# Loading the local attention's values 64 keys at a time for all heads, with the scores put to match and every step in a new order

## The chip, the cores and the metric

The kernel runs on one core of a Trainium2 chip. The metric is the device time of one execution in microseconds (us). The version before the change has a median of 604.21 us over three runs (601.29 to 608.74). One further execution was recorded by the hardware profiler; every duration of a single instruction below comes from that one.

The core has a matrix engine (PE), three elementwise engines (DVE, ACT and POOL) and a queue called SP, which in this kernel issues every DMA transfer. Each of the five works through its own instructions strictly in order, and waits on semaphores when an input is not there yet.

## What is computed

Two pieces follow one another: an attention with a pooled and a local part, and a feed-forward block (the "FFN").

```python
B, H, S, D = 8, 8, 576, 64
# pooled part: q, k, v averaged over 4 neighbouring positions
out_d  = softmax(q_d @ k_d.T / 8) @ v_d            # 144 x 144 a head
# local part: only keys with |i - j| < 4 count
scores = where(mask, q @ k.T / 8, -1e9)
out    = repeat(out_d, 4) + softmax(scores) @ v
x      = out.transpose(0, 2, 1, 3).reshape(4608, 512)
# FFN
h  = x @ w_in                                      # 512 -> 1024
so = h * softmax(h)
ln = (so - mean(so)) / sqrt(var(so) + 1e-6) * g_ln
return ln @ w_out                                  # 1024 -> 512
```

The weights arrive as 64-bit floats and are turned into 32-bit ones on the core.

## The kernel before

**Attention, local part.** The 576 query positions of a batch are cut into ten windows of 64 keys, and two neighbouring windows make a unit `u` (five units a batch). All eight heads of a unit are worked on together, as four pairs of heads (`pr`), each with an even and an odd head (`par`). In batches 0 to 2, and for the fifth unit of batches 3 to 7, class `Local` (L525) does one unit: scores on PE (L539), mask, maximum, subtraction, exp, sum and scaling on DVE, POOL and ACT, a transpose of the probabilities through PE (L580), a copy out of PSUM (L583), the product with v on PE (L590) and the addition to the output (L595). That makes 15 + 5 = 20 units. In batches 3 to 7 the first four units go through class `PairOfLocals` (L601), two units at once, whose probabilities are transposed by DMA and DVE.

**How v is laid out for it.** `load_vw` (L256) fills one tile of 128 partitions for a unit; there are five such buffers. For a `Local` unit it uses four transfers of 64 KB: the half of the partitions is `par ^ wi` (`wi` is the window, 0 or 1), so that each half holds the even heads of one window and the odd heads of the other. The scores are laid out to suit: row half `wi`, PSUM bank `par ^ wi`; after the transpose the row half is `par ^ wi`. For the units of `PairOfLocals` the same function already uses two transfers of 128 KB, one for each window, with all eight heads side by side; there the row half is the window.

**Attention, pooled part.** Class `Pooled` (L698) works on the averaged q, k and v; v for it is loaded by `load_vs` and `load_tail` (L274, L284) and summed by L451 and L454.

**FFN.** The 4608 rows are cut into 36 tiles of 128 rows. For a tile, `ffn_in` (L773) makes 24 matmuls of 512 columns into one PSUM buffer (L779; high and low parts of weights and rows, three products), then maximum (L787), exp (L791), product (L794), centring (L817 on ACT or L819 on DVE), a store to DRAM (L827, `u`) and a sum of squares on ACT (L836), which waits for that store. `ffn_back` (L853) reads it back in four transfers (L859, `v`), `ffn_ut` transposes it on DVE (L880) and splits it (L886, L889), and `ffn_out` (L896) makes 24 more matmuls into another single PSUM buffer (L903), which ACT empties (L910). The last tile transposes on PE instead.

**Weights.** Sixteen pieces of 512 KB are loaded by `Weights.load` (L325, the steps `wload`) and converted by ACT (L334), DVE (L340 to L349) and DVE or POOL.

**The order.** The kernel first lists all its work as 1847 numbered steps (`step` and `row`, L948 to L953). A step is a piece of one unit or tile: one group of matmuls, one elementwise operation, or one load. They are then issued in the sequence of the list `ORDER` (L26), so this list alone sets the order of every engine's queue, SP's too. A second list, `OTHER` (L116), names the steps that run on the second-choice engine instead of the usual one (DVE in place of POOL or ACT; for the clamp at L336 POOL in place of DVE).

Some step numbers, for following the order in the code:

| step | what it is |
|---|---|
| 237, 245, 253, 261 | loads of the weight pieces 12, 13, 14, 15 |
| 238 | first conversion step of weight piece 12 (ACT, L334) |
| 278 | store of FFN tile 0 (L827) |
| 407, 417 | v load of batch 1, unit 0; the product on PE that reads it |
| 1249, 1263 | v load of batch 5, unit 0; the product on PE that reads it |
| 1677, 1692 | v load of batch 7, unit 3; the product on PE that reads it |
| 1445, 1446 | q and k load of batch 6, pair 1; the first DVE transpose that reads it |

Of the kernel before, what the change touches and what calls it, by code (L numbers as in the profile page):

```python
# [10 lines left out]
F32 = mybir.dt.float32  # L11
# [113 lines left out]
def pooled_local_attention_then_solu_ffn(  # L125
# [10 lines left out]
    nc = tc.nc  # L136
    P = 128
# [16 lines left out]
    W = 64  # L154
# [17 lines left out]
    def rows(n):  # L172
        return slice(n * 64, n * 64 + 64)
# [891 lines left out]
```

## Time and profile before

| quantity | value |
|---|---|
| median of three runs | 604.21 us (601.29 to 608.74) |
| the profiled execution, its own time | 605.33 us |
| its span from first to last instruction | 603.5 us |
| mean granted PE clock over the span | 0.963 |
| ACT busy | 306.1 us |
| POOL busy | 308.1 us |
| DMA issues, all on SP | 732 |
| data moved by DMA | 99.70 MB |

The profiled execution lies 1.12 us above the median; 605.33 - 603.5 = 1.8 us of it lie around the span. Busy time counts an engine's own work; issuing a DMA is not counted as busy, so SP's load is read from its timeline. In a timeline row the first number is the start in us after the span's start, the second the time the merged instructions take, and a bracket at the end gives the idle time of that engine before it, with the instruction or transfer that ended it. "PEclk" or "granted clock" is the share of full speed that PE was given.

### The profile page before, as it was taken

To read this page: it belongs to the slowest core of one execution; us is meant where nothing else is said; L and a number is where in the kernel's file an instruction comes from. 1 tells how busy PE (TensorE), PEld (TensorE's weight loads), DVE (VectorE), ACT (ScalarE), POOL (GpSimd) and SP (SyncE) were. 2 spreads that over 40 slices of the span, in tenths; PEclk is the share of its full clock that TensorE was granted. 3 is DMA by queue.
4 is the path that set the end of the run, shared out by engine and by line. 5 is a ranking of instruction groups with operands and counts; after the bars stand their busy time and mean duration, and the time that the engine had idled before them with its cause. 6 is when DMAs were issued, how large, how long until landed. Compare 5 with 4: busy or idle time off the path is not lost.

```text
span 603.5 us, 16899 instructions
## 1 busy us (share of the span) xinstructions
PE 560.4 (93%) x6728; PEld 436.9 (72%) x6728; DVE 459.0 (76%) x716; ACT 306.1 (51%) x639; POOL 308.1 (51%) x457
## 2 busy tenths in 40 slices
PE   7877978799899999979989999998999999999996
PEld 4655656577677777757767777776877777787885
DVE  3999987999787888768877876777888867654641
ACT  2466763576544564544534654454534547342443
POOL 5476574657385374554635564544637523532111
PEclk9698998799899999989998999998999999999999
DMA  8998658876878677797587877667672642333230
GB/s 237 243 233 147 136 123 171 210 185 136 189 182 161 194 205 206 136 250 185 153 216 155 207 206 168 160 164 183 182 196 77 200 136 81 107 122 123 88 123 35
DMA packets 208271, 99.70 MB, mean 165 GB/s; under 512 B 164288, under 2 KB 194496, under 8 KB 208192
## 3 DMA queue, kind: packets, MB, share of 16 engines
q1 hardware_dynamic: 208192, 98.62, 65.1%
q8 instruction: 53, 0.87, 0.6%
q14 instruction: 26, 0.21, 0.1%
HBM read 65.54 MB, written 27.79 MB: 155 GB/s over the span
## 4 chain that ended last, share of the span: by engine, by line
PE 42%; DVE 16%; SPq 16%; DMA 12%; issue 6%; POOL 5%; ACT 2%; DVEq 0%; POOLq 0%; ACTq 0%
PE h L779 18%; PE o L903 18%; SPq L249 6%; SPq L666 4%; DMA w<-in_moe_w_out_dram 2%; DMA stage<-in_moe_w_in_dram 2%; SPq L859 2%; PE po L755 2%; DMA v<-u 2%; SPq L268 2%; DMA qm<-in_q_dram 1%; DVE nmx L787 1%; DMA u<-e 1%; DVE kd L381 1%; PE sd L717 1%
## 5 line engine op out<-in xcount | busy, mean ns | idle before, releaser
L903 PE MATMUL o<-wo_h,uh 128*128 128x512 f32 x288 | 118.1, 410 | 5.4 <-ACT osb L910 5.4
L779 PE MATMUL h<-wi_h,xh 128*128 128x512 f32 x288 | 119.7, 416 | 1.4 <-DVE e L794 1.4
L779 PE MATMUL h<-wi_l,xh 128*128 128x512 f32 x288 | 116.6, 405 | 0.0
L779 PE MATMUL h<-wi_h,xl 128*128 128x512 f32 x288 | 116.3, 404 | 0.0
L903 PE MATMUL o<-wo_l,uh 128*128 128x512 f32 x288 | 115.0, 399 | 0.0
L889 POOL TENSOR_TENSOR ul<-v,uh 128x512 fp32r<-128x512 f32 x46 | 60.8, 1325 | 53.2 <-ACT uh L886 41.9
L903 PE MATMUL o<-wo_h,ul 128*128 128x512 f32 x288 | 79.5, 398 | 0.0
L791 ACT ACTIVATE e<-h,nmx 128x1024 f32<-128x1024 f32 x36 | 40.1, 1115 | 68.4 <-DVE nmx L787 64.2
L903 PEld LDWEIGHTS o<-wo_h,uh 128*128 128x128 f32 x288 | 54.7, 190 | 21.0 <-ACT osb L910 6.2
L779 PEld LDWEIGHTS h<-wi_h,xh 128*128 128x128 f32 x288 | 56.0, 194 | 16.7 <-DVE e L794 2.0
L880 DVE STREAM_TRANSPOSE v<-v 128x512 f32<-128x512 f32 x70 | 46.5, 690 | 25.6 <-DMA v<-u 24.5
L779 PEld LDWEIGHTS h<-wi_h,xl 128*128 128x128 f32 x288 | 55.9, 194 | 14.0 <-DVE xl L937 0.3
L779 PEld LDWEIGHTS h<-wi_l,xh 128*128 128x128 f32 x288 | 56.0, 194 | 12.4
L903 PEld LDWEIGHTS o<-wo_h,ul 128*128 128x128 f32 x288 | 54.7, 190 | 13.3
L886 ACT ACTIVATE uh<-v 128x512 fp32r<-128x512 f32 x70 | 42.9, 623 | 41.0 <-DVE v L880 21.9
L903 PEld LDWEIGHTS o<-wo_l,uh 128*128 128x128 f32 x288 | 54.8, 190 | 11.9
L787 DVE TENSOR_REDUCE nmx<-h 128x1 f32<-128x1024 f32 x36 | 43.6, 1211 | 24.5 <-PE h L779 24.5
L794 DVE SCALAR_TENSOR_TENSOR e<-h,e 128x1024 f32<-128x1024 f32 x36 | 43.6, 1212 | 14.4 <-ACT e L791 14.4
L799 POOL TENSOR_SCALAR nmu<-su 128x1 f32<-128x1 f32 x36 | 8.5, 237 | 76.9 <-DVE e L794 75.7
L836 ACT ACTIVATE e<-e 128x1024 f32<-128x1024 f32 x35 | 36.8, 1052 | 20.5 <-DMA u<-e 20.5
L817 ACT ACTIVATE e<-e,nmu 128x1024 f32<-128x1024 f32 x24 | 27.6, 1148 | 32.2 <-POOL nmu L799 32.2
L910 ACT ACTIVATE osb<-o,s 128x512 f32<-128x512 f32 x36 | 24.5, 679 | 32.3 <-PE o L903 13.5
(122 smaller groups left out, 1042.7 us busy)
## 6 DMA issues: line engine op xcount, KB each, us to landing
u<-e SPq DMA_DIRECT2D x35, 512.0 KB, 3.3
v<-u SPq DMA_DIRECT2D x140, 128.0 KB, 3.4
out_dram<-osb SPq DMA_DIRECT2D x36, 256.0 KB, 2.9
vs<-in_v_dram SPq DMA_DIRECT2D x64, 128.0 KB, 3.6
qm<-in_q_dram SPq DMA_DIRECT2D x96, 72.0 KB, 2.9
km<-in_k_dram SPq DMA_DIRECT2D x96, 72.0 KB, 2.5
vw<-in_v_dram SPq DMA_DIRECT2D x80, 64.0 KB, 2.9
vw<-in_v_dram SPq DMA_DIRECT2D x40, 128.0 KB, 3.3
```

The source lines that it names most:

```text
L249: nc.sync.dma_start(t[nm][Q * 32:Q * 32 + 32, pr], src[b, 2 * pr + par, :, dh * 32:dh * 32 + 32].rearrange("(k t) d -> t k d", t=32),)
L779: nc.tensor.matmul(hps[:, n, :], src[:, cc, :], wt[:, cc, n * 512:(n + 1) * 512], start=(cc == 0 and src is xh and wt is wi_h), stop=(cc = ...
L787: nc.vector.tensor_reduce(out=nmx, in_=hf, op=ALU.max, axis=AX.X, negate=True)
L791: nc.scalar.activation(e, hf, AF.Exp, bias=nmx, scale=1.0, accum_out=se)
L794: nc.vector.scalar_tensor_tensor(out=e, in0=hf, scalar=1.0, in1=e, op0=ALU.mult, op1=ALU.mult, accum_out=su)
L817: nc.scalar.activation(e, e, AF.Identity, bias=nmu, scale=1.0)
L836: nc.scalar.activation(e0, e, AF.Square, accum_out=m2)
L880: nc.vector.transpose(vg, vg)
L886: nc.scalar.activation(uh, tp, AF.Copy)
L889: (usual if v is None else engine(usual, nc.vector)).tensor_tensor(out=ul, in0=tp, in1=uh.bitcast(F32), op=ALU.subtract)
L903: nc.tensor.matmul(o, src[:, j, :], wt[:, 4 * g + j, :], start=(g == 0 and j == 0 and src is uh and wt is wo_h), stop=(g == 1 and j == 3 a ...
L910: nc.scalar.activation(osb, o, AF.Copy, scale=s)
```

## The change

Three things change; the arithmetic doesn't.

First, `load_vw` always uses two transfers of 128 KB, one a window, with all eight heads side by side. For the 20 `Local` units this takes two transfers where there were four: 732 DMA issues in all become 692. The bytes stay the same, and so does the run of 256 bytes (one head's 64 values of one key) that each element of a transfer covers.

Second, the scores of a `Local` unit go to row half `par ^ wi` and PSUM bank `wi` (before: row half `wi`, bank `par ^ wi`), and the product with v reads row half `wi`. The number and size of the matmuls stay.

Third, `ORDER` is another sequence of the same 1847 steps, and `OTHER` another choice (79 steps where there were 78, of which 25 are in both).

```diff
     def load_vw(b, u):
-        vw = load.tile([P, 2, NPR, D], F32, tag="vw", name=f"vw_{b}_{u}", bufs=5)
-        if b >= PAIRED and u < 4:
-            vw = vw.rearrange("p a r d -> p (a r) d")
-            for wi in range(2):
-                s0 = starts[2 * u + wi]
-                nc.sync.dma_start(vw[rows(wi)], v[b, :, s0:s0 + W, :].rearrange("h s d -> s h d"))
-            return vw
-
-        for par in range(2):
-            for wi in range(2):
-                s0 = starts[2 * u + wi]
-                nc.sync.dma_start(
-                    vw[rows(par ^ wi), wi, :, :],
-                    v[b, par::2, s0:s0 + W, :].rearrange("h s d -> s h d"),
-                )
+        vw = load.tile([P, H, D], F32, tag="vw", name=f"vw_{b}_{u}", bufs=5)
+        for wi in range(2):
+            s0 = starts[2 * u + wi]
+            nc.sync.dma_start(vw[rows(wi)], v[b, :, s0:s0 + W, :].rearrange("h s d -> s h d"))
         return vw
...
                     nc.tensor.matmul(
-                        sc[rows(wi), par ^ wi, pr * W:(pr + 1) * W],
+                        sc[rows(par ^ wi), wi, pr * W:(pr + 1) * W],
                         bt.qT[rows(par), pr, s0:s0 + W], bt.kT[rows(par), pr, s0:s0 + W],
...
             for pr in range(NPR):
-                for row, par in TILES:
-                    wi = row ^ par
+                for wi, par in TILES:
                     nc.tensor.matmul(
-                        xp[rows(par), wi, pr, :], bt.vw[u][rows(row), wi, pr, :],
-                        plT[rows(row), pr, wi, a0[wi]:a0[wi] + nw], start=True, stop=True,
+                        xp[rows(par), wi, pr, :], bt.vw[u][rows(wi), 2 * pr + par, :],
+                        plT[rows(wi), pr, par ^ wi, a0[wi]:a0[wi] + nw], start=True, stop=True,
                     )
```

Of the two lists, which fill some hundred lines, these places matter below.

- Ahead of the load of weight piece 12 (step 237), SP has 98 DMA issues before the change and 49 after it; ahead of piece 15 (step 261) 103 and 34, of piece 14 (step 253) 128 and 65, of piece 13 (step 245) 133 and 116.
- PE has 318 steps in its queue; 243 of them stand within two places of where they stood, and the last 16 are the same in both.
- At the head of the list the loads of two weight pieces now stand ahead of the first load of q; before it was one.
- The v load of batch 5, unit 0 (step 1249) stands directly ahead of the product that reads it (step 1263), where 180 steps lay between them; that of batch 7, unit 3 (step 1677) three steps ahead of its product (step 1692), where 317 lay between; and the q and k load of batch 6, pair 1 (step 1445) directly ahead of its first transpose (step 1446), where 42 lay between.
- In `OTHER`, DVE gains five accumulations, four scalings of pair units, three scalings of the pooled part, two centrings, two clamps of weights and one scaling of a single unit, and loses four copies of transposed probabilities, two subtractions of pair units, one of a single unit, two sums of v, two low parts of FFN rows and one copy of q.

180 rows, old and new, of tables (ORDER, OTHER) are left out of this document.

## The prediction

> **What bounds the kernel now.** I read the page's busy shares first, then busy time by stage, then SP's, DVE's and ACT's timelines in the stage that stood out. From the page:
>
> ```profile
> span 603.5 us, 16899 instructions
> ...
> PE 560.4 (93%) x6728; PEld 436.9 (72%) x6728; DVE 459.0 (76%) x716; ACT 306.1 (51%) x639; POOL 308.1 (51%) x457
> ...
> DMA packets 208271, 99.70 MB, mean 165 GB/s; under 512 B 164288, under 2 KB 194496, under 8 KB 208192
> ...
> PE 42%; DVE 16%; SPq 16%; DMA 12%; issue 6%; POOL 5%; ACT 2%; DVEq 0%; POOLq 0%; ACTq 0%
> ```
>
> PE is 93% busy, so over the whole span at most 43 us of idle PE can be won. But the chain that ended last spends 16% of the span in SP's queue, issuing transfers. Where, the windows tell (time, then busy us of PE, weight loads, DVE, ACT, POOL; granted clock, DMA share, GB/s):
>
> ```profile
> 0.00:75.00 75.00, 60.17 (x1131) 44.01 (x1134) 63.58 (x108) 40.09 (x93) 43.46 (x46) 0.91 0.86 199
> 75.00:125.00 50.00, 39.92 (x562) 29.45 (x553) 42.33 (x67) 26.89 (x45) 30.76 (x35) 0.86 0.72 164
> 125.00:470.00 345.00, 332.06 (x4054) 261.19 (x4054) 277.09 (x425) 178.96 (x385) 192.89 (x284) 0.98 0.73 178
> 470.00:592.00 122.00, 121.86 (x971) 97.60 (x970) 74.56 (x116) 56.69 (x112) 39.65 (x89) 1.00 0.37 120
> 592.00:603.50 11.50, 6.37 (x29) 4.68 (x27) 1.45 (x3) 3.50 (x6) 1.32 (x5) 1.00 0.12 46
> ```
>
> From 125 us on PE is the bound: 12.9 us idle of 345, then 0.1 of 122. Since its work is fixed and its queue is full, whatever is won before 125 us is kept to the end. Before 125 us DVE is the busiest engine. From 75 to 125 PE lacks 10.1 us and DVE 7.7. What DVE waits for there:
>
> ```profile
> 90.75 1.22 DVE L794 SCALAR_TENSOR_TENSOR e<-h,e 128x1024 f32<-128x1024 f32 x1 [1.93 <-ACT e L791]
> ...
> 95.81 0.43 DVE L336 TENSOR_SCALAR w<-w 128x512 f32<-128x512 f32 x1 [3.83 <-ACT w L334]
> ...
> 115.83 0.43 DVE L336 TENSOR_SCALAR w<-w 128x512 f32<-128x512 f32 x1 [0.89 <-ACT w L334]
> ```
>
> These are 1.93 + 3.83 + 0.89 = 6.65 of the 7.7 us. ACT, which ends all three, waits in turn for DMA:
>
> ```profile
> 88.47 1.06 ACT L836 ACTIVATE e<-e 128x1024 f32<-128x1024 f32 x1 [2.87 <-DMA u<-e]
> ...
> 95.11 0.67 ACT L334 ACTIVATE w<-w 128x512 f32<-128x512 f32 x1 [3.39 <-DMA w<-in_moe_w_out_dram]
> ```
>
> The first holds back ACT's exp (L791), and through it DVE's L794. And the transfers are late because SP issues without a pause; here are its rows:
>
> ```profile
> 59.35 5.83 SPq L268 DMA_DIRECT2D vw<-in_v_dram  x8
> ...
> 75.67 9.68 SPq L268 DMA_DIRECT2D vw<-in_v_dram  x12
> 85.45 0.55 SPq L827 DMA_DIRECT2D u<-e  x1
> 86.09 2.61 SPq L268 DMA_DIRECT2D vw<-in_v_dram  x4
> 88.80 0.55 SPq L325 DMA_DIRECT2D w<-in_moe_w_out_dram  x1
> ...
> 91.34 0.38 SPq L325 DMA_DIRECT2D w<-in_moe_w_out_dram  x1
> 91.81 4.49 SPq L268 DMA_DIRECT2D vw<-in_v_dram  x4
> ...
> 109.50 0.60 SPq L325 DMA_DIRECT2D w<-in_moe_w_out_dram  x1
> ```
>
> Twelve v issues take 9.68 us ahead of the store of tile 0 at 85.45, four more stand ahead of a weight load at 88.80, and four (91.81) ahead of the one at 109.50. PE itself waits for v once:
>
> ```profile
> 89.09 0.37 PE L590 MATMUL xp<-plT,vw 64*64 64x58 f32 x2 [2.71 <-DMA vw<-in_v_dram]
> 90.17 1.43 PE L590 MATMUL xp<-plT,vw 64*64 64x58 f32 x30 [0.72 <-DMA vw<-in_v_dram]
> ```
>
> **The change, part by part. Fewer issues.** Issue durations (min/median/max in ns) of the 64 KB loads, then of the 128 KB loads that the other units have already:
>
> ```profile
> L268 SPq DMA_DIRECT2D vw<-in_v_dram x80: 595/615/1921, 30.8 to 456.1; - x80
> ```
>
> ```profile
> L262 SPq DMA_DIRECT2D vw<-in_v_dram x40: 595/634/2392, 197.1 to 472.8; - x40
> ```
>
> A larger transfer costs SP nearly the same, so a unit falls from 4 x 0.615 = 2.46 us to 2 x 0.634 = 1.27: 1.19 less, and 20 units give 23.8 us of SP time. In the rows above, from 59.35 to 88.70, stand 24 v issues, which are six units: SP would reach the weight load at 88.80 some 6 x 1.19 = 7.1 us earlier and, with five units by then, the store at 85.45 some 5.9 us earlier. Each is more than the wait that hangs on it (3.83 and 1.93), and by 109.50 the seven units of these rows have saved 8.3 us against 0.89. Moreover the new order puts weight pieces 12, 15 and 14 at 49, 34 and 65 issues from the head of SP's queue instead of 98, 103 and 128. So I let all three waits of DVE go: -6.65 us. What is late next is DVE's own work, which fills the rest of this stage (42.33 + 6.65 = 48.98 of 50 us), so PE can't win its whole 10.1 us. The bounds are 0 (something else ends these waits) and -10.1 (all of PE's idle time). PE's own 3.4 us for v lie at the same place as DVE's first two waits and are not added.
>
> The Trainium skill ("DMA: Bandwidth & Descriptors", section "Issuing engines are not separate DMA queues") says that sequencer time for starting transfers is usually small beside the transfer. By it this part is worth about nothing, and the time would stay at 604.2. The rows decide against it for this stage, where SP's issues stand back to back and other transfers queue behind them; the case is the first rival below.
>
> **Transfers themselves.** Time to landing of the larger loads, from the page's list of issues:
>
> ```profile
> vw<-in_v_dram SPq DMA_DIRECT2D x40, 128.0 KB, 3.3
> ```
>
> Bytes and 256-byte runs stay. I take 0, since v is loaded ahead of its use; where that cover is gone, PE waits for the issues and these 3.3 us, which is the last rival.
>
> **Scores put to match.** Two rows of the chain (start, us, what):
>
> ```profile
> 137.07 1.09 PE sc L539 x64
> ...
> 144.40 0.92 PE sd L717 x48
> ```
>
> Two score steps take 1.09 us, 17 ns a matmul record. In the new layout neighbouring matmuls use different row halves of PE but the same column half. The pooled scores (L717) already do that, at 19 ns a record with 144 columns instead of 64, so I take 0. If such neighbours did wait for each other a step would double: 20 x 0.55 = 11 us, a bound I hold unlikely. No row speaks for a gain: the 17 ns are already under L717's 19.
>
> **The second-choice list.** Counted over the list DVE has 17 steps more and 12 fewer. The largest kind is the scaling of a pair unit on DVE:
>
> ```profile
> L656 DVE TENSOR_TENSOR pl<-pl,mxl 128x1024 f32<-128x1024 f32 x2 | 2.4, 1208 | 0.0
> ```
>
> Five net steps at no more than 1.21 us are at most +6 us of DVE work over the whole kernel. In the part of the list that runs up to 125 us it is one step fewer, and after 125 us DVE is idle 345 - 277 = 68 us: cost 0, and +6 if that cover were gone.
>
> **The new order.** PE's queue hardly moves (243 of 318 steps within two places), so its work ahead of each FFN tile is the same. At the head, one more 512 KB weight load stands ahead of the first q: 0.52 MB at 199 GB/s is 2.6 us that q comes later, or that DVE starts converting weights earlier; I take 0, bounds +2.6 and -2.6. After 125 us the 12.9 us of PE idle and, at clock 0.98, some 7 us of slower clock are stalls that a new order may heal or make. I see no sign which, and take 0; bounds -20 (all healed) and +21 (three new stalls, priced below).
>
> **Sum.** 603.5 - 6.65 = 596.9 us of span, 605.33 - 6.65 = 598.7 for this execution; it lay 1.1 above the median, so against the median 604.21 - 6.65 = 597.6 us.
>
> **The rivals.** *Nothing comes of it, 604.2 us.* The waits end with transfers, not with their issue: if the DMA engines are the limit, the same bytes land as late as before. For it: the DMA share of 0.86 up to 75 us, and 164288 of 208271 packets under 512 B, which stay. The Trainium skill (the same page, "Specifications") asks for at least 512 B a transfer to reach line rate, and this change leaves 256. Against it: the share is only 0.72 from 75 to 125, and SP, not a transfer, is what the late store and weights queue behind.
>
> *The steady stage heals too, about 587.6 us.* A freer SP queue, 10 issues fewer after 200 us, and a new order remove half of the 20 us of stalls and slow clock: 597.6 - 10 = 587.6. From 5.5 us on it is faster by over 2%. For it: SP's 16% of the chain is more than this one stage. Against it: only 10 of the 40 issues lie there.
>
> *Loads too close to their use, 616.8 us.* Steps 1249, 1677 and 1445 now stand right ahead of what reads them. If SP is no longer ahead there, PE waits for two issues and the landing, 1.27 + 3.3 = 4.6 us, and the slower clock adds 7 / 12.9 of that: 7.0 us. Less what such a stall would overlap, 6.4. Three of them give 597.6 + 3 x 6.4 = 616.8; one alone leaves the forecast, two bring back the time before, the third decides. For it: the wait at 89.09 is such a case (step 407 stood three places ahead of 417). Against it: SP often runs ahead of the list's place, and three must miss.
>
> **How the numbers follow.** Forecast (start stage wins, steady stage as before) 0.52, its own range 592 to 603; nothing comes of it 0.18; steady stage heals 0.16; loads too close 0.14, of which over half stays below the third stall. About 2% (592.1 and 616.3) is what a measurement of this kernel can tell from no change. Faster by over 2%: 0.16 and a sliver of the forecast, 0.17. Slower: 0.06 of the last rival and 0.02 for doubled score steps, 0.08. Within: 0.75. The range 588 to 611 leaves out about half of the second and half of the third rival.
>
> **What would show it.** Right: 20 units with two v issues of about 0.63 us; DVE's waits on ACT L334 and L791 between 75 and 125 us gone, and its busy time there near 49 of 50 us; the stage from which PE is over 95% busy begins near 118 instead of 125 us; L539 still 1.09 us for two steps. Wrong: PE stalls on v in batches 5 or 7, DVE waiting on batch 6's k, or weights still late behind other transfers.

## The result and the profile after

The changed kernel takes 577.07 us (median of four runs, 576.53 to 577.40), the kernel before 604.56 us beside it (601.29 to 608.74). The ratio is 0.954, with a 95% interval of 0.948 to 0.960: faster, by some 27 us where 6.65 had been forecast. The time lies below the predicted range. The profiled execution took 576.97 us with a span of 575.2 us and a mean granted clock of 0.991.

From the page of the changed kernel:

```profile
span 575.2 us, 16860 instructions
...
PE 544.7 (95%) x6728; PEld 422.1 (73%) x6728; DVE 460.3 (80%) x720; ACT 304.2 (53%) x637; POOL 303.5 (53%) x455
...
DMA packets 207631, 99.70 MB, mean 173 GB/s; under 512 B 163648, under 2 KB 193856, under 8 KB 207552
...
PE 78%; DVE 8%; DMA 5%; SPq 4%; issue 2%; ACT 2%; POOL 1%; POOLq 0%; DVEq 0%; ACTq 0%
```

SP's queue has gone from 16% to 4% of the chain that ended last. The span fell by 603.5 - 575.2 = 28.3 us. Of these, 560.4 - 544.7 = 15.7 us are PE's busy time, with the same 6728 matmuls: they ran at a higher clock. The other 12.6 us are idle time of PE.

Where it went, by stage of the changed kernel (columns as in the prediction: time, then busy us of PE, weight loads, DVE, ACT, POOL; granted clock, DMA share, GB/s):

```profile
0.00:75.00 75.00, 55.96 (x1122) 39.53 (x1126) 62.94 (x109) 41.52 (x94) 40.37 (x44) 0.93 0.95 222
75.00:125.00 50.00, 44.05 (x719) 32.66 (x709) 47.70 (x80) 35.84 (x69) 37.27 (x42) 1.00 0.83 186
125.00:470.00 345.00, 344.20 (x4209) 270.14 (x4208) 295.40 (x447) 182.52 (x390) 198.65 (x304) 1.00 0.72 181
470.00:563.00 93.00, 92.95 (x664) 74.16 (x663) 52.84 (x85) 40.58 (x80) 26.12 (x64) 1.00 0.35 117
```

Two stages won. From 75 to 125 us DVE works 47.70 of 50 us where it worked 42.33, and PE 44.05 where it worked 39.92. From 125 to 470 us PE lacks 0.80 us of 345 at clock 1.00, where it lacked 12.94 at 0.98. The prediction had put a gain on the first stage and none on the second.

In the first stage, DVE's waits for ACT's conversions and exp are gone from the timeline. Of idle times before DVE's rows, the timeline from 75 to 125 us shows only one, for another reason:

```profile
116.77 0.71 DVE L868 STREAM_TRANSPOSE v<-v 128x512 f32<-128x512 f32 x1 [1.65 <-DMA v<-u]
```

In the second stage, the view of waits from 125 to 470 us names what PE waited for (us in total, times, longest). Before:

```profile
PE o L903 <- ACT osb L910: 4.1, 1, 4.1
PE sc L620 <- DVE qT L427: 2.4, 2, 1.5
PE po L755 <- POOL vd L454: 2.3, 1, 2.3
PE po L755 <- DVE pd L746: 1.6, 1, 1.6
PE h L779 <- DVE e L794: 1.1, 1, 1.1
PE sd L717 <- DVE pl L626: 1.1, 1, 1.1
...
```

After:

```profile
PE sc L608 <- DVE pl L614: 0.3, 1, 0.3
PE sc L608 <- DVE r L818: 0.3, 1, 0.3
PE plt L569 <- DVE pl L560: 0.2, 1, 0.2
```

The stalls of over 1 us had six different causes, so no single engine or transfer was at fault. What else changed shows one step further back, in DVE's waits in the same stretch. Those for DMA before:

```profile
DVE v L880 <- DMA v<-u: 19.2, 10, 3.8
DVE kT L423 <- DMA km<-in_k_dram: 8.2, 3, 4.1
...
DVE plT L671 <- DMA plT<-pl: 5.6, 3, 2.1
```

and after:

```profile
DVE v L868 <- DMA v<-u: 1.8, 1, 1.8
```

Before, DVE waits 33.0 us here for transfers, 19.2 of them for FFN tiles on their way back to the transposes. In the changed kernel it waits 1.8 us. ACT's waits for the stores of these tiles, before it squares them, fall too; first before, then after:

```profile
ACT e L836 <- DMA u<-e: 16.0, 7, 5.6
```

```profile
ACT e L824 <- DMA u<-e: 1.2, 1, 1.2
```

Whether these waits are the cause is the question of the last experiments.

**A measure used below.** PE's order hardly differs between the kernels, so their progress can be compared at equal work. PE's lag at a mark of 120 us is the time at which it starts the step that has 120 us of PE's own work before it in the queue, less 120; each step counts at the duration it has at full clock. The mark of 120 is reached at 156.4 us before the change and at 146.6 after it, so what is lost up to it belongs to the start; what the lag grows from 120 to 500 belongs to the steady stage. Only differences between kernels are read from it: the lag of the changed kernel grows by 14.8 us too, though its PE is idle for only 0.80 us between 125 and 470 us, so most of that growth is in the way the steps are counted and no loss.

### The profile page after: what moved, and what is told of

It reads as the page before. It is cut to its first block, busy times and chain, and to the rows that moved or that the text cites. A ratio compares the mean times of both kernels' runs of the same rounds, so it can differ in the third digit from the quotient of the medians.

```text
span 575.2 us, 16860 instructions
## 1 busy us (share of the span) xinstructions
PE 544.7 (95%) x6728; PEld 422.1 (73%) x6728; DVE 460.3 (80%) x720; ACT 304.2 (53%) x637; POOL 303.5 (53%) x455
## 2 busy tenths in 40 slices
DMA packets 207631, 99.70 MB, mean 173 GB/s; under 512 B 163648, under 2 KB 193856, under 8 KB 207552
## 4 chain that ended last, share of the span: by engine, by line
PE 78%; DVE 8%; DMA 5%; SPq 4%; issue 2%; ACT 2%; POOL 1%; POOLq 0%; DVEq 0%; ACTq 0%
PE o L891 32%; PE h L767 30%; SPq L249 3%; PE po L743 3%; PE xp L666 2%; DMA km<-in_k_dram 2%; PE sc L608 2%; PE sd L705 2%; DMA qm<-in_q_dram 1%; PE qp L485 1%; PE plt L569 1%; PE warm L948 1%; PE kp L485 1%; PE xp L578 1%; DVE w L334 1%
## 5 line engine op out<-in xcount | busy, mean ns | idle before, releaser
L767 PE MATMUL h<-wi_h,xh 128*128 128x512 f32 x288 | 116.7, 405 | 0.3 <-DVE e L782 0.3
L767 PE MATMUL h<-wi_h,xl 128*128 128x512 f32 x288 | 113.9, 396 | 0.0
L767 PE MATMUL h<-wi_l,xh 128*128 128x512 f32 x288 | 113.9, 395 | 0.0
L877 POOL TENSOR_TENSOR ul<-v,uh 128x512 fp32r<-128x512 f32 x48 | 64.1, 1340 | 42.2 <-ACT uh L874 35.4
L767 PEld LDWEIGHTS h<-wi_h,xh 128*128 128x128 f32 x288 | 54.1, 188 | 14.6 <-issue 0.9
L891 PEld LDWEIGHTS o<-wo_h,ul 128*128 128x128 f32 x288 | 53.8, 188 | 14.1 <-POOL ul L877 0.9
L767 PEld LDWEIGHTS h<-wi_h,xl 128*128 128x128 f32 x288 | 54.1, 188 | 13.2 <-POOL xl L925 0.2
L767 PEld LDWEIGHTS h<-wi_l,xh 128*128 128x128 f32 x288 | 54.1, 188 | 12.0
L898 ACT ACTIVATE osb<-o,s 128x512 f32<-128x512 f32 x36 | 24.5, 680 | 50.1 <-PE o L891 16.9
L925 POOL TENSOR_TENSOR xl<-x,xh 128x512 fp32r<-128x512 f32 (+1 forms) x26 | 32.0, 1233 | 21.1 <-ACT xh L922 20.7
L805 ACT ACTIVATE e<-e,nmu 128x1024 f32<-128x1024 f32 x22 | 25.2, 1146 | 22.5 <-POOL nmu L787 22.5
```

What stands on the lines that cost most here:

```text
L767: nc.tensor.matmul(hps[:, n, :], src[:, cc, :], wt[:, cc, n * 512:(n + 1) * 512], start=(cc == 0 and src is xh and wt is wi_h), stop=(cc = ...
L805: nc.scalar.activation(e, e, AF.Identity, bias=nmu, scale=1.0)
L877: (usual if v is None else engine(usual, nc.vector)).tensor_tensor(out=ul, in0=tp, in1=uh.bitcast(F32), op=ALU.subtract)
L891: nc.tensor.matmul(o, src[:, j, :], wt[:, 4 * g + j, :], start=(g == 0 and j == 0 and src is uh and wt is wo_h), stop=(g == 1 and j == 3 a ...
L898: nc.scalar.activation(osb, o, AF.Copy, scale=s)
L925: engine(nc.gpsimd, nc.vector).tensor_tensor(out=l, in0=src, in1=h.bitcast(F32), op=ALU.subtract)
```

## Experiments

All times are medians; the ratio is to runs of the kernel before on the same chip (603 to 607 us), with its 95% interval. The last two columns are PE's lag as just described, from each one's profiled execution.

| kernel | us | ratio | lag at 120 | growth 120 to 500 |
|---|---|---|---|---|
| before | 604.56 | 1 | 36.4 | 33.2 |
| changed | 577.07 | 0.954 [0.948, 0.960] | 26.6 | 14.8 |
| e1, loads and layout alone | 592.59 | 0.983 [0.979, 0.988] | 31.1 | 25.6 |
| e2, order and layout, four loads | 588.09 | 0.976 [0.971, 0.981] | 37.4 | 15.7 |
| e3, order alone | 588.25 | 0.977 [0.972, 0.983] | 36.6 | 15.9 |
| e4, new order, old `OTHER` | 612.07 | 1.017 [1.011, 1.022] | 32.5 | 43.6 |
| e5, SP's queue from the new order | 643.68 | 1.062 [1.055, 1.069] | 33.9 | 73.4 |
| e6, SP's queue from the old order | 658.26 | 1.088 [1.082, 1.094] | 39.6 | 82.4 |
| e7, old order, new `OTHER` | 610.01 | 1.008 [1.005, 1.012] | 34.5 | 39.7 |
| e8, one load moved | 592.84 | 0.978 [0.973, 0.983] | 31.4 | 27.8 |
| e9, old head, new rest | 582.68 | 0.960 [0.955, 0.966] | 32.6 | 15.1 |
| e10, new head, old rest | 589.52 | 0.973 [0.969, 0.977] | 29.5 | 25.2 |
| e11, old half, new rest | 586.64 | 0.968 [0.964, 0.972] | 30.3 | 21.2 |
| e12, q ahead of a weight | 579.85 | 0.961 [0.956, 0.965] | 28.5 | 14.1 |
| e13, tiles fetched earlier, old order | 599.44 | 0.989 [0.985, 0.995] | 31.6 | 33.8 |
| e14, tiles fetched late, new order | 633.05 | 1.045 [1.041, 1.050] | 33.7 | 48.0 |
| e15, e13 and later squares | 597.53 | 0.988 [0.982, 0.994] | 29.9 | 29.2 |

### Which of the three parts?

e1 has the two loads and the new layout with the lists `ORDER` and `OTHER` of before; e2 has the new lists and layout, but the 20 single units load v in four transfers; e3 has the new lists with the old code; e4 has the new order with the old `OTHER`. The edit of e2 to the changed kernel:

```diff
-            nc.sync.dma_start(vw[rows(wi)], v[b, :, s0:s0 + W, :].rearrange("h s d -> s h d"))
+            for hh in range(0, H, 4 if b < PAIRED or u == 4 else 8):
+                n = 4 if b < PAIRED or u == 4 else 8
+                nc.sync.dma_start(
+                    vw[rows(wi), hh:hh + n], v[b, hh:hh + n, s0:s0 + W, :].rearrange("h s d -> s h d")
+                )
```

> The old order and the old second-choice list, with two v transfers a unit and the new layout of the scores. Theory A (the fewer issues on SP are what wins in the start stage, and the new order healed the stalls after 125 us): the start stage wins its 7 to 10 us, so 595 to 598 us, and the four stalls after 125 us (before L620 at 159, L903 at 262, L755 at 315 and L755 at 412 us) stay. Theory B (the order does nearly all of it): 601 to 605 us. Theory C (the freer SP queue also heals the stalls after 125 us): 577 to 585 us.

> The new order and layout, but each of the 20 single units loads v in four transfers of 64 KB again (each window's heads 0 to 3, then 4 to 7), so that SP issues 732 transfers. Theory A: the start stage loses 7 to 10 us again, the rest stays healed: 584 to 587 us. Theory B: 577 to 579 us. Theory C: 595 us or more.

> The new order and second-choice list with the old load and the old layout of the scores. If the layout costs and brings nothing, the same as the run with four loads and the new layout, within 1.5 us. If the new layout of scores and PSUM banks is faster or slower in itself, the two differ by up to 11 us (20 score steps at 0.55 us).

> The new order, loads and layout with the old second-choice list. If which engine does a step is free where the engines have idle time: 577 to 579 us. If the list is part of what healed the stalls: 582 us or more, with new waits of PE for DVE, ACT or POOL.

The loads alone give 603.31 - 592.59 = 10.7 us, the order alone 15.1, and both 27.5 by their own comparison: nearly the sum. The time of e1 lies in none of the three ranges that were expected of it, but between those of theories A and C; that of e2 lies 1 us above theory A's. The layout costs nothing (588.09 with it, 588.25 without). The lags show where each part works: the loads alone win 5.3 us in the start and 7.6 in the steady stage, the order alone nothing in the start (36.6 against 36.4) and 17.3 in the steady stage. With the new order the loads win nearly all of theirs in the start (37.4 to 26.6) and little in the steady stage (15.7 to 14.8). The windows agree. From 125 to 470 us, with the loads alone:

```profile
125.00:470.00 345.00, 334.23 (x4135) 263.49 (x4136) 284.19 (x435) 181.93 (x380) 197.35 (x291) 1.00 0.73 183
```

and with the order and four loads:

```profile
125.00:470.00 345.00, 340.10 (x4251) 266.63 (x4250) 294.43 (x448) 183.66 (x393) 197.11 (x299) 1.00 0.73 183
```

e4 then shows that the order heals nothing unless `OTHER` goes with it: 35 us are lost, most of them in the steady stage. This is so although DVE hardly waits for transfers there. From 125 to 470 us e4 has only this wait of DVE for one:

```profile
DVE v L868 <- DMA v<-u: 2.9, 3, 1.2
```

So these waits go with the sequence of the list, but they don't measure by themselves what is lost: e4 has 2.9 us of them and a growth of 43.6 us, e1 has 31.4 us of them and a growth of 25.6, the kernel before 33.0 and 33.2.

### The list of second choices, and SP's queue by itself

e7 is e1 with the new `OTHER`. e5 and e6 mix the two orders: in e5 SP's queue follows the new order and the other engines the old one, in e6 the reverse. Where that would block, a load was taken forward (6 of SP's 247 steps in e5, 3 in e6). The diff of e5 to e1 at its first lines:

```diff
 ORDER = """
-4 141 14 22 21 142 32 143 144 145 40 42 43 146 147 148 24 26 165 166 34 167 168 169 27 157 158
+4 14 22 21 165 141 142 143 144 145 40 32 42 43 146 147 148 157 24 26 166 34 167 168 169 27 158
...
```

> Two v transfers a unit; PE, DVE, ACT and POOL in the old order with the old second-choice list, but SP's queue in the new order (6 of its 247 steps had to come earlier than there, because the old order needs them sooner). The same with SP in the old order took 592.6 us. Theory S (the stalls after 125 us were transfers that came late behind others in SP's queue, and the new SP order healed them): 577 to 582 us. Theory E (the elementwise engines' and PE's own orders healed them): 590 us or more.

> Two v transfers a unit; PE, DVE, ACT and POOL in the new order with the new second-choice list, but SP's queue in the old order (3 of its 247 steps had to come earlier). Theory S: the stalls come back, 590 to 595 us. Theory E: 577 to 580 us. If the two kinds of order only work together: both this run and the one with the queues the other way round above 590 us.

> Two v transfers a unit, the old order with the new second-choice list (592.6 us with the old list). The new order with the old list took 612.1 us, 35 us more than with its own. If a list only fits the order it was made with: 605 us or more, with PE waiting in new places behind steps that stand in another engine's queue. If the old list was simply worse: 585 to 592 us.

Neither side carries the gain alone: with SP's queue taken from the other order, either way round, the kernel is slower than before, by 6 and 9%. That is the case that e6's expectation names last, that the two only work together. How much of the gain belongs to either side can't be told from such mixtures. The new `OTHER` in the old order costs 610.0 - 592.6 = 17.4 us. Each of the two lists fits its own order only. The likely reason, which no run isolates, is that each engine's queue is in order: a step put on another engine stands behind other steps there, and its reader gets it at another time; that DVE has idle time says nothing of that.

### One stall taken away

In e1 the largest stall of PE in the steady stage is this one, and ACT's rows show why (PE's row first):

```profile
252.47 0.50 PE L891 MATMUL o<-wo_h,uh 128*128 128x512 f32 x1 [2.77 <-ACT osb L898]
```

```profile
250.18 1.06 ACT L824 ACTIVATE e<-e 128x1024 f32<-128x1024 f32 x1 [3.58 <-DMA u<-e]
251.14 0.18 ACT L824 ACTIVATION_READ_ACCUMULATOR e<-e 128x1 f32 x1
251.23 0.61 ACT L551 ACTIVATE pl<-pl 128x512 f32<-128x512 f32 x1
251.75 0.67 ACT L898 ACTIVATE osb<-o,s 128x512 f32<-128x512 f32 x1
```

ACT waits for a tile's store before it squares it; the copy that frees PE's buffer stands behind that in ACT's queue. The store was late, because SP issued q and k loads, and one fetch of a tile, before it (229.54 to 246.97 us, then the store at 247.07). e8 is e1 with one of these loads (step 1228, eight issues) moved behind a later store:

```diff
-... 1228 ... 748 ...
+... 748 1228 ...
```

> The old order and list with two v transfers a unit (592.6 us), and one step moved in SP's queue: the q and k load of batch 5, pair 1 (8 issues, about 5.2 us) now stands behind the store of FFN tile 10 instead of ahead of it. Theory S: the 2.8 us that PE waited for ACT L898 near 252 us go, and with them the 3.4 us at half clock behind it: 588 to 590 us. Theory E: the stall stays and the time too, 592 to 593 us.

The stall at 252 us is gone, and the time is the same, 592.84 against 592.59 us. Others took its place, such as this one, before the moved load:

```profile
188.83 0.80 PE L767 MATMUL h<-wi_h,xh 128*128 128x512 f32 x1 [2.50 <-DVE e L782]
```

It is not shown that the moved load made these. e8's runs spread from 586.6 to 595.3 us, more than the 3 to 5 us that theory S expected, and the profiled one took 594.95, so the run can't rule out a small gain. The chain behind one stall can be read from the trace; that taking it away would win its length can't, and here it didn't show.

### Where along the list the gain is made

e9 has the first 450 steps of the old order (PE passes there near 125 us), then the other steps in the sequence of the new one. e10 is the reverse. e11 is e9 with the seam after step 1000, near 290 us. `OTHER` goes with the part; all have two loads. For e9:

```diff
 ORDER = """
-165 141 40 22 166 167 168 169 42 170 171 172 142 143 144 4 32 34 43 145 157 158 159 146 147 24
+4 141 14 22 21 142 32 143 144 145 40 42 43 146 147 148 24 26 165 166 34 167 168 169 27 157 158
...
```

> Two v transfers a unit and the new score layout; the first 450 steps of the list as in the order before (PE reaches their end near 125 us), the other 1397 in the sequence of the new order; OTHER goes with each part. Theory H (the gain of the order is made in the steady stage, by the new sequence there alone): PE's lag behind its own work grew after 140 us of PE work by 22.6 us in the old order with two loads and by 12.7 us in the changed kernel, so this kernel takes 592.6 - 9.9 = 582.7 us, 579 to 586. Theory R (the new head sets the queues up so that the steady stage runs without stalls): the stalls stay, 590 to 595 us. Theory J (a list fits only as a whole, and any seam costs): over 597 us.

> The other way round: two v transfers a unit and the new score layout; the first 450 steps in the new order, the rest in the sequence of the order before, OTHER with each part. Theory H: only what the new head wins is won, 592.6 - 5.4 = 587.2 us (5.4 is the difference of PE's lag at 140 us of PE work, 34.1 with the old order and two loads against 28.7 in the changed kernel), 585 to 590. Theory R: near the changed kernel, 577 to 582 us. Theory J: over 597 us.

> As the kernel with the old head and the new rest, but the seam after step 1000 of the list, where PE has done 243 of its 500 us of work (about 290 us into the run). Theory H, with the gain spread over the stage: by then the old order's lag is 43.5 us (between 37.9 at 200 and 45.1 at 260 us of PE work) and the new sequence adds 41.4 - 33.4 = 8 us to the 500 us mark where the old one adds 56.7 - 43.5 = 13.2, so 592.6 - 5.2 = 587.4 us, 584 to 591. Theory R: 590 to 595 us. Theory J: over 597 us.

Theory H holds in all three, 582.7, 589.5 and 586.6 us, and the other two don't. That 582.7 is met to the tenth is luck: the kernel before took 607.41 us beside these three and 603.31 beside e1, from which the expectations start. The ratios keep the same sequence, 0.983 for e1, then 0.973 (e10), 0.968 (e11), 0.960 (e9) and 0.954 for the changed kernel. The seam costs nothing that can be seen. With the old head, the steady stage is as free of stalls as in the changed kernel:

```profile
125.00:470.00 345.00, 343.40 (x4309) 269.59 (x4303) 296.06 (x446) 183.72 (x390) 197.45 (x301) 1.00 0.73 182
```

and with the new head and the old rest it isn't:

```profile
125.00:470.00 345.00, 337.42 (x4060) 265.68 (x4060) 283.26 (x432) 179.22 (x377) 194.85 (x289) 0.98 0.71 178
```

So the steady gain is made by the sequence within that stage, in both halves of it (e11 has about half), and does not hang on how the queues stand when it begins.

### The head of the list

e12 is the changed kernel with the second weight load behind the first two loads of q:

```diff
-165 141 40 22 166 167 168 169 42 170 171 172 142 143 144 4 32 34 43 145 157 158 159 146 147 24
+141 40 32 165 22 166 167 168 169 42 170 171 172 142 143 144 4 34 43 145 157 158 159 146 147 24
```

> The changed kernel, but at the head of SP's queue the load of weight piece 3 (512 KB) stands behind the first two loads of q instead of ahead of them; nothing else moves. If q's arrival sets the pace of the head (PE waits 4.46 us for the first q in the changed kernel, 1.73 in the one before), the gap shrinks by about 2.7 us and is kept to the end: 577.1 - 2.7 = 574.4 us. If DVE, which is the busier engine there and has piece 3 to convert first, sets the pace, DVE loses what PE wins: 577.1 to 579.7 us.

It takes 579.85 us (578.13 to 582.97), 2.8 more than the changed kernel, whose runs all lie below these. The two were measured beside different runs of the kernel before (605.54 and 604.56 us), and the intervals of their ratios overlap, so that it is slower is likely but not certain. The first theory falls, and the second fits: PE waits 3.5 us for its first q instead of 4.5, but DVE waits for the first weight

```profile
DVE w L325 <- ACT w L323: 6.5, 1, 6.5
```

in the first 40 us, where its longest such wait was 2.6 us. What PE wins at the head is lost again at DVE.

### Is it the distance between a fetch and its reader?

In e13, the old order with two loads, 18 of the `ffn_back` loads stand further ahead of the DVE transpose that reads them (the expectations call it a copy). In e14, the changed kernel, each of the 35 stands directly ahead of it. e15 is e13 with six of ACT's squares later. For tile 8 (load 599, first transpose 600) in e13:

```diff
-... 745 581 857 599 600 580 ...
+... 1061 1062 742 599 1094 892 ... 745 581 857 600 580 ...
```

> Old order with two v transfers (592.6 us), but the 18 loads bringing an FFN tile back from DRAM (ffn_back) that stood less than 4 us of PE work ahead of the DVE copy that reads them stand up to 7 us ahead of it; two of them find hardly any room. Theory D (the new order heals the steady stage because what comes back over DMA is asked for earlier before its reader, so that DVE doesn't wait and hold up what is queued behind): between 125 and 470 us DVE waits 18.2 us for these loads in the old order with two loads and 1.8 us in the changed kernel; here it falls under 8 us. They are 18.2 of DVE's 31.4 us of waits for DMA there and of some 70 us over DVE, ACT and POOL, so 26 to 58% of the 9.9 us between the two orders in this stage: 587 to 590 us. Rival S (these waits are idle time that PE doesn't see): the waits go and the time stays, 592.6 within 2 us. Rival M (any move costs): over 595 us.

> The changed kernel, with each of the 35 ffn_back loads moved to stand directly ahead of the DVE copy that reads it; nothing else moves. Theory D: DVE's waits for these loads between 125 and 470 us come back (1.8 us in the changed kernel, 18.2 in the old order), to 15 us or more, PE's stalls of over 1 us come back, and the time rises by 3 to 10 us: 580 to 587 us. Rival S: the waits come back and the time stays, 577.1 within 1.5 us.

> As the kernel with the 18 loads moved earlier, and ACT's square of a tile (which waits for the tile's store) moved later in ACT's queue for the six tiles where it stood less than 5 us of PE work behind the store. Theory D: ACT's wait for the store (13.2 us between 125 and 470 us in the old order with two loads) falls under 6 us too; with 31.4 of some 70 us of waits gone, 45% of 9.9: 585 to 589 us, below the kernel with the loads alone. Rival S: 592.6 within 2 us.

Taking the distance away is ruinous: 633.05 us, 56 more than the changed kernel, far above the 3 to 10 expected. In e14, from 125 to 470 us, DVE waits

```profile
DVE v L868 <- DMA v<-u: 31.7, 7, 10.8
```

and PE stalls behind it, the longest here:

```profile
181.16 0.80 PE L767 MATMUL h<-wi_h,xh 128*128 128x512 f32 x1 [8.24 <-DVE e L782]
```

The rival, that PE doesn't see these waits, falls. But giving the old order the distance doesn't heal it: e13 takes 599.44 us and e15 597.53, no better than e1 and rather worse (ratios 0.989 and 0.988 against 0.983). So rival M, that any move costs, has the number for e13; e8, where a moved load cost nothing, speaks against it as a rule. DVE's waits for the tiles fell only from 18.2 to 12.8 us in e13, and all its waits for transfers together are 33.0 us against 31.4 in e1. ACT's wait for the stores, which e15 was to take away, is 13.3 us there against 13.2 in e1. Neither run reached what its theory asked for, so they don't show what would come of it if these waits did go. SP's own waits in the same stretch show what the move of e13 did instead. In e1:

```profile
SPq L847 <- DMA u<-e: 6.1, 5, 2.3
```

In e13:

```profile
SPq L847 <- DMA u<-e: 16.3, 6, 4.8
```

L847 is the fetch, which has to wait for the tile's store. Moved forward, it waits in SP's queue, and everything queued behind it waits too: DVE's waits for k (L412) rise from 5.0 to 10.5 us. The wait has only changed queues. So a distance of the fetch from its reader is needed for the new order's gain (e14), and moving the fetch alone doesn't bring the gain (e13).

What the new order does differently can be counted in the lists. These are medians over the 35 tiles, in places of `ORDER` and not in time:

| `ORDER` | product (L794) to store | store to fetch | fetch to DVE's transpose |
|---|---|---|---|
| old | 18 | 24 | 13 |
| e13 | 18 | 18 | 19 |
| new | 30 | 23 | 19 |

e13 gave the fetch the new order's distance to its reader, but took it from the room that the store has. In the new order the whole chain from the product on is longer. The difference is one of the median alone: within three places of its reader stand 7 of the 35 fetches in the old order and 8 in the new. That the steps ahead of the fetch (the centring, the store) have to be early as well is a reading of these runs and counts; no run moves the whole chain.

It stays open which moves of the new order make the gain. None of the runs is faster than the changed kernel.

## Why the prediction was wrong

**Fewer issues: right in its mechanism, with a term left out.** A unit's v goes out in two issues that are hardly longer (min/median/max in ns):

```profile
L260 SPq DMA_DIRECT2D vw<-in_v_dram x80: 595/634/2197, 31.4 to 479.7; - x80
```

DVE's waits for L334 and L791 went, and its busy time from 75 to 125 us is 47.70 us (forecast: near 49). PE is over 95% busy only from 125 us on, as before, and not from 118: from 115 to 125 us it works 8.47 of 10 us. The sum went by idle time alone and left out the clock in this stage. Before the change two stretches of 6.8 us at about half clock (from 89.17 and 113.06 us) lie in it, in e1 and in the changed kernel none: the granted clock from 75 to 125 us goes from 0.86 to 1.00. In e1 PE's busy time there rose only from 39.92 to 40.85 us, so most of what the loads win in this stage is clock. The term was -6.65 us with bounds of 0 and -10.1. Measured in the start, the loads are worth 5.3 us in the old order (e1) and 37.4 - 26.6 = 10.8 in the new one (changed kernel against e2). What was missed is that they help in the steady stage too where that still stalls, by 7.6 us in e1. The Trainium skill ("DMA: Bandwidth & Descriptors", section "Issuing engines are not separate DMA queues") calls the sequencer's time for a start usually small beside the transfer. For a single load the trace agrees, 0.63 us against 3.4 us to landing. But here one queue issues everything, one load behind the other, and with 40 issues fewer and the same bytes e1 is 10.7 us faster.

**Nothing comes of it: wrong.** 163648 packets under 512 B are left, and the time fell all the same.

**Scores and layout: right.** 0 was taken; e2 and e3 differ by 0.2 us. A score matmul is as long as before, first before and then after:

```profile
L539 PE MATMUL sc<-kT,qT x640: 213/218/367, 27.1 to 435.9; 64*64 64x64 f32 x160
```

```profile
L528 PE MATMUL sc<-kT,qT x640: 217/218/366, 22.0 to 407.0; 64*64 64x64 f32 x160
```

**The new order: the step that failed.** "I see no sign which, and take 0; bounds -20 (all healed) and +21." The steady stage healed almost entirely: 33.2 - 14.8 = 18.4 us by the lag, of which the order alone makes 17.3 (e3). The bound was right and the value wrong: there was no reason for 0 beyond the lack of a sign. The rival "the steady stage heals too" had the mechanism, at half the price and with a chance of 0.16; it put the gain down to a freer SP queue and weighed it by the 10 issues saved after 200 us. With the loads unchanged (e3) the order heals as much. The sum made from the measured lags is 604.2 - 9.8 - 18.4 = 576.0 us, against 577.1 measured. What within the new sequence does it stays open, as said above.

There was a sign that could have been read blind, though it would not have given the size: DVE's 33 us of waits for DMA in a stage where PE's 12.9 us of idle time had six different causes. The places of each product, store, fetch and reader in the two lists, as counted above, would have leaned towards a gain; that they would have settled it is not shown. The prediction checked only PE's queue (243 of 318 steps nearly in place) and three v and k loads that had come closer to their readers.

**Loads too close: wrong.** In the changed kernel no wait of PE from 125 to 470 us ends with a transfer. The view puts one wait of ACT (L898, 4.1 us once) down to a v load, but that line reads no v, so it is no sign of a late one.

**The second-choice list: wrong as argued.** It was priced by DVE's idle time, at 0 to +6 us. In its own order no cost is seen, but with the wrong order it costs 17 (e7) and the old one 35 us (e4). The two lists are one change, not two terms.

**The head: within its bounds.** One more weight ahead of q was taken as 0 with bounds of 2.6 us either way; undoing it takes 2.8 us more (e12), hardly clear of noise, so it was a small gain if any.

## What to carry to other kernels

Where in-order queues feed one another and a list sets their order, that order can be a term as large as the engine time it leaves idle: bound it by idle time and slow clock of the bound engine, then look in the list at the places of product, store, fetch and reader before choosing a value inside the bounds. Ask what a transfer itself waits for: in e13 moving the fetches alone moved the wait into the issuing queue, where it held up unrelated loads. Here order and engine choice that were found together had to be kept together.

## What the runs showed of the hardware

PE's busy time fell by 15.7 us with the same matmuls. The trace's clock records have eight stretches at about half clock before the end of the run in the kernel before, 3.4 to 10.2 us long and 44.4 us in all, and three of 3.4 us in the changed kernel; half of the 34.1 us between them is 17 us. Between 125 and 470 us of the kernel before there are four of them (from 160.84, 263.24, 314.44 and 413.43 us), and each begins within 1 us of the end of one of PE's waits of 1.46 to 4.12 us; the wait of 2.33 us that ends at 314.88 us goes with 6.8 us at half clock. So a stall can cost more than its length. Not each does: one of 1.14 us (at 181.15 us) has no slow stretch beside it. And SP's price for an issue of v depends hardly on its size, 615 ns for 64 KB and 634 ns for 128 KB.
